# A fused attention and gate kernel: gate by exp and reciprocal in the last steps, a moved V group, an earlier K set, a split copy

## The chip, the cores and the metric

The kernel runs on one core of a Trainium2 chip. Its time is that of one execution in device microseconds, as the median of several runs. Every engine works through its own instructions in order: PE (TensorE, matrix products), ACT (ScalarE), DVE (VectorE), POOL (GpSimd) and SP (which only issues DMAs here).

## The reference

For one sequence of 2048 rows of width 512, with 32 heads of 16 and an inner width of 1376:

```python
xn = _layernorm(x, axis=-1)
s = _A_ref(xn, A_wqkv, A_wo)           # 32 heads: softmax(q k^T / 4) v, then @ wo
h = _gelu(jnp.einsum("bsd,df->bsf", xn, w1) + b1)
g = _silu(jnp.einsum("bsf,fd->bsd", h, w2) + b2)
return x + s * g
```

All is fp32. `silu(y)` is `y / (1 + exp(-y))`.

## The kernel before

**Precision.** Most products are made of three: each operand is split into a high part (rounded by an ACT copy) and a low part (the rest, by a subtraction on POOL or DVE), and high x high, high x low and low x high are added up in PSUM (`mm3`, L73 to 79, and `terms`).

**Work units.** The 2048 rows are 16 token tiles of 128 (`t`), or four chunks of 512 (`c`). Heads go in eight groups of four. A unit `u` is one head group and one chunk of queries, so there are 32 units of 16 key tiles each, that is 512 attention steps (`n`).

**First part (to about 57 us).** Layer norm, transposes, the first Q and K rows, and one V tile per chunk.

**Stage one (about 57 to 490 us).** A list (`plan`, L238 to 257) is built by a small planner and then carried out. Its entries are: three groups of four V tiles (`quad`), then up pairs and Q/K pairs, each in two halves (`half`), with the down products of finished up tiles between them (`down`). `half` accumulates a pair in the banks `ps_x` and `ps_m` and hands it to `evac` (gelu or copy on ACT, the split on ACT and POOL). `BANKS` says which PSUM pools a V group takes. When a chunk's down products are complete, its four gate tiles are copied to `gt` (L571) and put in `chores` and `silu`. `chore` adds `b2` on POOL. `gate` (L584 to 593), called behind the next Q/K pair, applies Silu to the four tiles on ACT and stores them to `g_d` in DRAM from POOL's queue; a gelu on a dummy element follows. Gelu, Silu, Exp and Sqrt each need a table in ACT, and the build puts a table load ahead of a function whose table is not there. The last chunk's four tiles are stored without Silu.

**Scores, for the softmax's maximum.** A score tile (S, `s_one`, L161 to 180) is one matmul of 48 rows into a bank of `s_tile` and a maximum over its 512 columns on DVE (L175). Each unit has 64 of them. In stage one `fill` (L466) puts S between the other matmuls, so that `4 * LEAD` of the 2048 S are done at its end. The rest are spread over the attention steps: `due(n)` (L791) says how many must be done by step `n`, in one straight line up to step `KBACK` and in a second one up to step `DONE`; 768 are due at `KBACK`. `KBACK` is thus the step from which the fourth K set (head group 3) is used, which is loaded into the place of the first in two halves, at steps 57 and 64, from POOL's queue.

**Attention steps (about 490 to 1619 us).** Each step makes four score products again (T, `t_one`, L691), now with the maximum subtracted inside the product, takes exp of each on ACT (L700), and multiplies the previous step's four results with V (V, `pv_step`, L702 to 716, eight matmuls). The order of T, S and V in a step is written out by hand for each number of S (`ORDER`, L39):

```python
ORDER = {0: "TTTTV", 1: "TTTTSV", 2: "TTTSTSV", 3: "STTTSTSV", 4: "STTSTSVTS"}
```

T uses four PSUM banks in turn, S three, V one. Behind the last V of a unit its result is copied out of that one bank to `os` (L712 to 716); the next unit's first V needs the bank. `o_move`, `o_den` and `o_div` then bring the sums to the denominators' place, take their reciprocals on DVE (L734), spread them through DRAM and divide (L744; on POOL, for the last unit on DVE).

`at(n, f, ...)` (L784) hangs further work on a step: loads of Q and K, `load_gx` (a token tile's `g` and `x`, from SP's queue, into four buffers `gx`), `w_token` (the split of a token tile's attention result), `w_mul` (its product with `wo`, four times 3 matmuls over two steps) and `w_out` (L776: times `g` on DVE, plus `x` on POOL, stored by SP). From step `DONE` on (490) there are no S any more, and the token tiles 0 to 10 are finished there, two steps each. Behind the loop come tile 11 (`spare`) and the last chunk's four, `T3` = 12 to 15. Two of those have their result split by chunk (`w_chunk`) in steps 509 and 511. In the tail the last unit is divided, and Silu is applied to the `g` of tiles 12 to 15 on ACT (L860 to 868).

Of the kernel before, what the change touches and what calls it, by code (L numbers as in the profile page):

```python
# [8 lines left out]
F32 = mybir.dt.float32  # L9
# [7 lines left out]
P = 128  # L17
# [14 lines left out]
VW = DH + 1  # L32
LEAD = 140
DONE = 490
KBACK = 70
FILL0 = 84
# [4 lines left out]
XB = 6  # L41
BANKS = ("ttvt", "xmtt", "ttvt")


@with_exitstack
def fused(ctx: ExitStack, tc: tile.TileContext, x, wqk, wv, wo, w1, b1, w2, b2, out):
# [101 lines left out]

    halves = [[(u, st, p) for u in range(NU) for st in range(NCH * NCH) for p in range(2)] for _ in range(2)]
    made = [0, 0]  # L150
# [86 lines left out]
    is_m = [pair[0][0] == "m" for pair in pairs]  # L237
    plan, nd = [("first", g) for g in range(VQ)], 0  # L238
    for j in range(len(pairs)):
        for h in range(2):  # L240
            plan.append(("half", j, h))
            ready = 4 * sum(is_m[:j])
            due = next((i for i in range(j, len(pairs)) if is_m[i]), len(pairs))
            nxt = next((i for i in range(j + h, len(pairs)) if is_m[i]), len(pairs))
            left = 2 * (nxt - j) + 1 - h
            need = 4 * sum(is_m[:nxt]) - 4 - nd
            room = 2 * (due + 1 - j) - h
            n = 2 if nd < len(parts) and parts[nd][2] and ready - nd > room else 1
# [290 lines left out]

    PA, silu, chores = {}, [], []  # L540

    def down(c, f, part):
# [22 lines left out]
        if f == FT - 1:  # L565
            for t in range(NCH):
                gt = wk.tile([P, D], F32, name="gt", bufs=4)
                if c == NCH - 1:
                    nc.vector.tensor_add(gt, PA[c][t], b2_sb)
                else:  # L570
                    nc.scalar.activation(gt, PA[c][t], AF.Copy)  # L571
                    chores.append(gt)
                rs = slice(c * CH + t * P, c * CH + (t + 1) * P)
                if c < NCH - 1:
                    silu.append((gt, rs))
                else:
                    nc.gpsimd.dma_start(g_d[rs, :], gt)

    def chore():
        if chores:  # L580
            gt = chores.pop(0)
            nc.gpsimd.tensor_add(gt, gt, b2_sb)

    def gate():  # L584
        while chores:
            chore()
        if not silu:
            return
        while silu:
            gt, rs = silu.pop(0)  # L590
            nc.scalar.activation(gt, gt, AF.Silu)
            nc.gpsimd.dma_start(g_d[rs, :], gt)
        nc.scalar.activation(junk, ident_r[:1, :1].bitcast(F32), AF.Gelu_apprx_tanh)

# [5 lines left out]
    def half(j, h):  # L600
# [5 lines left out]
        else:  # L606
            run((terms(y, 0, False), terms(x, 1, False)), {2: [lambda: w1_load(j + 2), errand], 10: [chore]})
            evac((x, y), PH)
            if x[0] == "q":
                gate()  # L610

    def quad(n):
# [4 lines left out]
        for i in range(4):  # L617
            hooks = {6: [mark]} if i in (1, 2) else {}
            if n == VQ - 1 and i in (0, 2):
                hooks[3] = [lambda: w1_split(0) if i == 0 else w1_load(1)]  # L620
# [81 lines left out]
    def pv_step(u, k):  # L702
# [8 lines left out]
        if k == NT - 1:  # L711
            OS[u] = wb.tile([P, CH], F32, name="os", bufs=1)  # L712
            if u < NU - 1:
                nc.scalar.activation(OS[u], PV.pop(u), AF.Copy)  # L714
            else:
                nc.vector.tensor_copy(OS[u], PV.pop(u))

# [27 lines left out]

    GX, OTS, PW = {}, {}, {}

    def load_gx(t):
        GX[t] = wb.tile([P, 2, D], F32, name="gx", bufs=4)
        nc.sync.dma_start(GX[t][:, 0], g_d[t * P:(t + 1) * P, :])  # L750
        nc.sync.dma_start(GX[t][:, 1], x[t * P:(t + 1) * P, :])

    def w_round(blocks, src, lo):
# [60 lines left out]
    for t in range(spare):  # L814
        n = DONE + 2 * t
        at(n - 4, load_gx, t)
        at(n - 2, w_token, t)
        at(n, w_mul, t, KS[:2])
        at(n + 1, w_mul, t, KS[2:])
        at(n + 1, w_out, t, nc.gpsimd)  # L820
    at(L - 4, load_gx, spare)
    at(L - 2, w_token, spare)
    for i, t in enumerate(T3[:2]):
        at(L - 3 + 2 * i, load_gx, t)
        at(L - 3 + 2 * i, w_chunk, i, nc.vector if i else nc.gpsimd)
    for k in range(KT):
        at(104 + 16 * k, load_wo, k)
        at(112 + 16 * k, split_wo, k)
# [76 lines left out]
```

## Time and profile before

| | |
|---|---|
| time, median of 3 runs | 1650.65 us (1649.59 to 1656.22) |
| time of the profiled execution | 1649.32 us |
| its span, first to last instruction | 1647.2 us |
| granted TensorE clock, mean | 0.996 |
| PE busy | 1624.7 us (99%) |
| DVE busy | 1371.6 us (83%) |
| ACT busy | 1284.8 us (78%) |
| POOL busy | 366.6 us (22%) |

The profile records one execution. A row of it names a line of the kernel, an engine, an operation, the tile written and those read, and the durations. Times in rows are microseconds from the span's start. Where rows of the same kind follow each other they are merged, with their count behind an x; what stands in brackets is the idle time of the engine ahead of the row and the instruction that ended it. PE's rows overlap, as matmuls are pipelined, so the distance from start to start is the measure there.

### The profile page before, as it was taken

To read this page: it belongs to the slowest core of one execution; us is meant where nothing else is said; L and a number is where in the kernel's file an instruction comes from. 1 tells how busy PE (TensorE), PEld (TensorE's weight loads), DVE (VectorE), ACT (ScalarE), POOL (GpSimd) and SP (SyncE) were. 2 spreads that over 40 slices of the span, in tenths; PEclk is the share of its full clock that TensorE was granted. 3 is DMA by queue.
4 is the path that set the end of the run, shared out by engine and by line. 5 is a ranking of instruction groups with operands and counts; after the bars stand their busy time and mean duration, and the time that the engine had idled before them with its cause. 6 is when DMAs were issued, how large, how long until landed. Compare 5 with 4: busy or idle time off the path is not lost.

```text
span 1647.2 us, 30938 instructions
## 1 busy us (share of the span) xinstructions
PE 1624.7 (99%) x11624; PEld 891.4 (54%) x11624; DVE 1371.6 (83%) x2256; ACT 1284.8 (78%) x2564; POOL 366.6 (22%) x360
## 2 busy tenths in 40 slices
PE   8999999999999999999999999999999999999997
PEld 7889989989984333333333343433333333433444
DVE  7289989999988888888888888988888888888612
ACT  4333443543539999999999999999999999999874
POOL 4145565756640011001000100100100000000143
PEclk9999999999999999999999999999999999999999
DMA  5635333463431122111411411411141111110243
GB/s 199 130 89 149 107 120 104 131 165 93 133 116 35 28 48 50 28 43 38 70 31 27 70 38 28 63 34 29 38 62 28 28 28 40 29 29 21 75 131 133
DMA packets 76069, 116.82 MB, mean 71 GB/s; under 512 B 24948, under 2 KB 25972, under 8 KB 74552
## 3 DMA queue, kind: packets, MB, share of 16 engines
q1 hardware_dynamic: 72464, 102.30, 22.9%
q0 software_dynamic: 3264, 12.35, 4.3%
q8 instruction: 92, 1.51, 0.4%
q14 instruction: 57, 0.47, 0.1%
q10 hardware_dynamic: 192, 0.20, 0.0%
HBM read 84.35 MB, written 25.97 MB: 67 GB/s over the span
## 4 chain that ended last, share of the span: by engine, by line
PE 93%; ACT 2%; DVE 1%; DMA 1%; issue 1%; POOL 1%; SPq 0%; ACTq 0%; DVEq 0%; POOLq 0%
PE pv L708 30%; PE ps L173 25%; PE ps L491 11%; PE pst L698 11%; PE pst L491 7%; PE ps L698 3%; PE ps L76 3%; PE pv L491 2%; ACT slot L700 1%; PE pst L76 1%; DMA xt<-in_x 0%; DMA raw<-in_wqk 0%; DMA gx<-in_x 0%; DVE slot L71 0%; PE ps L366 0%
## 5 line engine op out<-in xcount | busy, mean ns | idle before, releaser
L175 DVE TENSOR_REDUCE mx<-ps 128x1 f32<-128x512 f32 x2048 | 1306.5, 684 | 178.9 <-PE ps L173 68.1
L700 ACT ACTIVATE slot<-pst 128x512 f32<-128x512 f32 x1536 | 840.4, 611 | 44.2 <-PE pst L698 22.2
L708 PE MATMUL pv<-slot,vsb 128*32 128x512 f32 x4096 | 545.2, 604 | 1.4 <-ACT os L714 1.3
L173 PE MATMUL ps<-kt,slot 48*128 48x512 f32 x1024 | 368.2, 441 | 0.0
L698 PE MATMUL pst<-qt,kt 50*128 50x512 f32 x1152 | 358.8, 434 | 0.7 <-ACT slot L700 0.2
L173 PEld LDWEIGHTS ps<-kt,slot 48*128 48x128 f32 x1024 | 185.6, 184 | 275.0 <-DVE mx L175 256.6
L700 ACT ACTIVATE slot<-ps 128x512 f32<-128x512 f32 x512 | 312.6, 611 | 10.0 <-PE ps L173 1.9
L491 PE MATMUL ps<-slot,w1h 64*128 64x512 f32 x1088 | 227.9, 397 | 3.6 <-ACT junk L501 2.7
L173 PE MATMUL ps<-kt,qz 48*128 48x512 f32 x512 | 210.4, 415 | 0.3
L698 PEld LDWEIGHTS pst<-qt,kt 50*128 50x128 f32 x1152 | 162.3, 185 | 44.2 <-ACT slot L700 16.9
L173 PE MATMUL ps<-slot,slot 48*128 48x512 f32 x512 | 185.7, 438 | 0.0
L708 PEld LDWEIGHTS pv<-slot,vsb 128*32 128x32 f32 x4096 | 80.6, 108 | 182.6 <-issue 169.9
L698 PE MATMUL ps<-qt,kt 50*128 50x512 f32 x384 | 165.4, 431 | 0.0
L491 PEld LDWEIGHTS ps<-slot,w1h 64*128 64x128 f32 x1088 | 153.6, 186 | 15.7 <-ACT junk L501 5.6
L173 PEld LDWEIGHTS ps<-slot,slot 48*128 48x128 f32 x512 | 93.2, 184 | 126.4 <-DVE mx L175 117.0
L491 PE MATMUL ps<-slot,w1l 64*128 64x512 f32 x544 | 151.2, 395 | 0.0
L301 POOL TENSOR_TENSOR hl<-hg,hh 128x512 fp32r<-128x512 f32 x76 | 96.9, 1297 | 134.0 <-ACT hh L300 89.6
L698 PE MATMUL pst<-qt,slot 50*128 50x512 f32 x384 | 118.7, 432 | 0.0
L188 POOL TENSOR_TENSOR nmh<-nm,nmh 128x16 fp32r<-128x16 f32 x32 | 7.1, 222 | 492.4 <-DVE nm L187 364.2
L501 ACT ACTIVATE junk<-ident_r 1x1 f32<-1x1 f32 x95 | 18.6, 196 | 118.1 <-PE pv L491 74.9
L173 PEld LDWEIGHTS ps<-kt,qz 48*128 48x128 f32 x512 | 94.1, 184 | 11.8 <-DVE mx L175 3.4
L491 PEld LDWEIGHTS ps<-slot,w1l 64*128 64x128 f32 x544 | 85.1, 187 | 4.1
(143 smaller groups left out, 1648.9 us busy)
## 6 DMA issues: line engine op xcount, KB each, us to landing
raw<-in_w SPq DMA_DIRECT2D x88, 256.0 KB
qk_h<-hh SPq DMA_DIRECT2D x32, 256.0 KB
qk_l<-hl SPq DMA_DIRECT2D x32, 256.0 KB
qt<-qk_h SPq DMA_DIRECT2D x128, 64.0 KB
slot<-qk_h SPq DMA_DIRECT2D x96, 64.0 KB
xt<-in_x SPq DMA_DIRECT2D x16, 256.0 KB
g_d<-gt POOLq DMA_DIRECT2D x16, 256.0 KB, 4.2
qt<-qk_l SPq DMA_DIRECT2D x64, 64.0 KB
```

Of the source, the lines that this page charges most:

```text
L76: nc.tensor.matmul(ps, lhs[a], rhs[b], start=first and n == 0, stop=last and n == 2)
L173: nc.tensor.matmul(ps, q[r, p, qi * P:(qi + 1) * P], kts[g % KB][p][r, ki * CH:(ki + 1) * CH], start=True, stop=True)
L175: nc.vector.tensor_reduce(MX[u][:, 2 * p + a, qi, ki:ki + 1], ps, axis=AX.X, op=OP.max)
L188: nc.gpsimd.tensor_sub(NM[u][:, 1], nm, NM[u][:, 0].bitcast(F32))
L301: nc.gpsimd.tensor_sub(hl, raw, hh.bitcast(F32))
L491: i = nc.tensor.matmul(ps, lhs[r], rhs[r], start=first, stop=last).ins
L501: i = nc.scalar.activation(junk, ident_r[:1, :1].bitcast(F32), AF.Copy).ins
L698: nc.tensor.matmul(ps, kts[g % KB][p][r, k * P:(k + 1) * P], QT[u][r, p, :], start=True, stop=True)
L700: nc.scalar.activation(PT[u, k][:, 2 * p + a, :], ps, AF.Exp, scale=SCALE)
L708: nc.tensor.matmul(PV[u][32 * j:32 * j + 32, :], vsb[:, k, h:h + 32], PT[u, k][:, j, :], start=(k == 0), stop=(k == NT - 1))
```

## The change

1. `LEAD` 140 to 145 (580 S instead of 560 in stage one) and `KBACK` 70 to 64. The unit that first uses the fourth K set does its S in another order: first all that need the first half of the key columns.
2. Two of the three V groups come ahead of the first up pair, the third behind it. The second group takes its banks in another order.
3. The gates are no longer finished in stage one: `chore` adds `b2` and stores at once, and Silu is gone. Instead, `gate(t)` in the last steps computes `g / (1 + exp(-g))` per token tile: exp on ACT into one of four buffers (by `t % 4`), then plus one, reciprocal and product on DVE. It is hung on the step of `w_token` for tiles 0 to 11, on steps 505 and 507 for tiles 12 and 13, and on the tail for 14 and 15, between `o_den` and `w_out(spare)`. The `gx` of tiles 12 and 13 gets places of its own (in slots that held a K set) and is loaded in steps 501 and 503, that of tile 14 in step 511, that of tile 15 in the tail.
4. The copy at the end of a unit is half on ACT, half on DVE, for all units.

```diff
-LEAD = 140
+LEAD = 145
 DONE = 490
-KBACK = 70
+KBACK = 64
...
-BANKS = ("ttvt", "xmtt", "ttvt")
+BANKS = ("ttvt", "xtmt", "ttvt")
...
-    halves = [[(u, st, p) for u in range(NU) for st in range(NCH * NCH) for p in range(2)] for _ in range(2)]
+    def score_order(u):
+        tiles = list(range(NCH * NCH))
+        return sorted(tiles, key=lambda st: st % NCH // 2) if u == NCH * KB else tiles
+
+    halves = [[(u, st, p) for u in range(NU) for st in score_order(u) for p in range(2)] for _ in range(2)]
...
-    plan, nd = [("first", g) for g in range(VQ)], 0
+    plan, nd = [("first", g) for g in range(VQ - 1)], 0
     for j in range(len(pairs)):
         for h in range(2):
             plan.append(("half", j, h))
+            if j == 0 and h == 1:
+                plan.append(("first", VQ - 1))
...
                 else:
                     nc.scalar.activation(gt, PA[c][t], AF.Copy)
-                    chores.append(gt)
                 rs = slice(c * CH + t * P, c * CH + (t + 1) * P)
                 if c < NCH - 1:
-                    silu.append((gt, rs))
+                    chores.append((gt, rs))
...
     def chore():
         if chores:
-            gt = chores.pop(0)
+            gt, rs = chores.pop(0)
             nc.gpsimd.tensor_add(gt, gt, b2_sb)
-
-    def gate():
-        while chores:
-            chore()
-        if not silu:
-            return
-        while silu:
-            gt, rs = silu.pop(0)
-            nc.scalar.activation(gt, gt, AF.Silu)
             nc.gpsimd.dma_start(g_d[rs, :], gt)
-        nc.scalar.activation(junk, ident_r[:1, :1].bitcast(F32), AF.Gelu_apprx_tanh)
...
             evac((x, y), PH)
-            if x[0] == "q":
-                gate()
...
-            if n == VQ - 1 and i in (0, 2):
+            if n == VQ - 2 and i in (0, 2):
                 hooks[3] = [lambda: w1_split(0) if i == 0 else w1_load(1)]
...
-            if u < NU - 1:
-                nc.scalar.activation(OS[u], PV.pop(u), AF.Copy)
-            else:
-                nc.vector.tensor_copy(OS[u], PV.pop(u))
+            pv = PV.pop(u)
+            nc.scalar.activation(OS[u][:, :CH // 2], pv[:, :CH // 2], AF.Copy)
+            nc.vector.tensor_copy(OS[u][:, CH // 2:], pv[:, CH // 2:])
...
+    def spare_slot(i):
+        while len(spares) <= i:
+            spares.append(slot(len(spares), (P, KT, D)))
+        return spares[i]
+
     def load_gx(t):
-        GX[t] = wb.tile([P, 2, D], F32, name="gx", bufs=4)
+        if t in T3[:2]:
+            i = 2 * T3.index(t)
+            GX[t] = spare_slot(1)[:, i:i + 2]
+        else:
+            GX[t] = wb.tile([P, 2, D], F32, name="gx", bufs=4)
         nc.sync.dma_start(GX[t][:, 0], g_d[t * P:(t + 1) * P, :])
         nc.sync.dma_start(GX[t][:, 1], x[t * P:(t + 1) * P, :])
+
+    def gate(t):
+        e, g = spare_slot(0)[:, t % NCH], GX[t][:, 0]
+        nc.scalar.activation(e, g, AF.Exp, scale=-1.0)
+        nc.vector.tensor_scalar_add(e, e, 1.0)
+        nc.vector.reciprocal(e, e)
+        nc.vector.tensor_mul(g, g, e)
...
         at(n - 2, w_token, t)
+        at(n - 2, gate, t)
...
     at(L - 2, w_token, spare)
+    at(L - 2, gate, spare)
     for i, t in enumerate(T3[:2]):
-        at(L - 3 + 2 * i, load_gx, t)
+        at(L - 11 + 2 * i, load_gx, t)
+        at(L - 7 + 2 * i, gate, t)
         at(L - 3 + 2 * i, w_chunk, i, nc.vector if i else nc.gpsimd)
+    at(L - 1, load_gx, T3[2])
...
     w_chunk(2, nc.vector)
-    load_gx(T3[2])
+    load_gx(T3[3])
     for k in KS[1:-1]:
         for t in T3:
             w_mul(t, (k,))
-    for t in T3[:2]:
-        nc.scalar.activation(GX[t][:, 0], GX[t][:, 0], AF.Silu)
     o_den(NU - 1)
+    for t in T3[2:]:
+        gate(t)
     w_out(spare, nc.gpsimd)
-    load_gx(T3[3])
-    nc.scalar.activation(GX[T3[2]][:, 0], GX[T3[2]][:, 0], AF.Silu)
     o_div(NU - 1, nc.vector)
     w_chunk(KT - 1, nc.vector)
-    nc.scalar.activation(GX[T3[3]][:, 0], GX[T3[3]][:, 0], AF.Silu)
```

More of the change, by code (lines that the diff above doesn't have):

```diff
@@ L538, in terms @@
         return out
-    PA, silu, chores = {}, [], []
+    PA, chores = {}, []
     def down(c, f, part):
@@ L744, in o_div @@
         eng.tensor_mul(ot[c][rs, g // 2], ot[c][rs, g // 2], DN.pop(u)[rs])
-    GX, OTS, PW = {}, {}, {}
-    def load_gx(t):
-        GX[t] = wb.tile([P, 2, D], F32, name="gx", bufs=4)
+    GX, OTS, PW, spares = {}, {}, {}, []
+    def spare_slot(i):
+        while len(spares) <= i:
+            spares.append(slot(len(spares), (P, KT, D)))
+        return spares[i]
+    def load_gx(t):
+        if t in T3[:2]:
[3 more added lines that the diff above has]
+            GX[t] = wb.tile([P, 2, D], F32, name="gx", bufs=4)
         nc.sync.dma_start(GX[t][:, 0], g_d[t * P:(t + 1) * P, :])
         nc.sync.dma_start(GX[t][:, 1], x[t * P:(t + 1) * P, :])
+    def gate(t):
[4 more added lines that the diff above has]
+        nc.vector.tensor_mul(g, g, e)
     def w_round(blocks, src, lo):
```

## The prediction

> **What bounds the kernel now.** I read the page first, then busy time by stage, then the instructions in order of time around each place that the change touches.
>
> ```profile
> PE 1624.7 (99%) x11624; PEld 891.4 (54%) x11624; DVE 1371.6 (83%) x2256; ACT 1284.8 (78%) x2564; POOL 366.6 (22%) x360
> ...
> L175 DVE TENSOR_REDUCE mx<-ps 128x1 f32<-128x512 f32 x2048 | 1306.5, 684 | 178.9 <-PE ps L173 68.1
> ```
> ```profile
> 57.00:489.60 432.60, 427.98 (x3529) 385.14 (x3525) 374.02 (x578) 175.34 (x386) 236.29 (x201) 1.00 0.42 118
> 489.60:1619.30 1129.70, 1127.73 (x7766) 452.14 (x7765) 952.99 (x1580) 1076.24 (x2116) 101.81 (x128) 1.00 0.20 45
> 1551.00:1619.30 68.30, 68.30 (x379) 31.68 (x378) 7.07 (x11) 49.49 (x97) 29.02 (x24) 1.00 0.36 116
> 1619.30:1647.20 27.90, 18.36 (x84) 12.53 (x82) 9.94 (x14) 7.54 (x12) 6.33 (x5) 0.89 0.41 135
> ```
> In the second fence the columns are the stretch, its length, then PE, weight loads, DVE, ACT and POOL, then the granted clock and the DMA share. PE is never out of work before 1619 us, so a gain must shorten PE's own sequence or remove one of its waits. In the attention steps (489.6 to 1619) ACT is also at 95% and DVE at 84%. In the part from 1551 on, where the scores are done, DVE is nearly idle: 7.07 of 68.30 us. That idle room is where the new gates go. In the last 28 us PE waits on others for a third of the time: there the chain counts, not the sum of work.
>
> The profiled execution took 1649.3 us for a span of 1647.2; the median of the runs is 1650.65. I sum against 1649.3. A measurement of this kernel can tell about 0.5% (8 us) from no change.
>
> **1. Fewer steps with four score tiles (LEAD, KBACK).** From the formula of the due scores: before, 20 of the steps hold four score tiles (S), 2 hold two; after, 2 hold four and 4 hold two. Twenty S move to stage one. One four-S step, with the start of its value matmuls (V) and the ones beside it:
> ```profile
> 1273.76 1.06 PE L708 MATMUL pv<-slot,vsb 128*32 128x512 f32 x8
> 1275.64 1.06 PE L708 MATMUL pv<-slot,vsb 128*32 128x512 f32 x8
> 1278.37 1.07 PE L708 MATMUL pv<-slot,vsb 128*32 128x512 f32 x8
> ```
> ```profile
> 1217.67 1.06 PE L708 MATMUL pv<-slot,vsb 128*32 128x512 f32 x8
> 1219.80 1.07 PE L708 MATMUL pv<-slot,vsb 128*32 128x512 f32 x8
> 1222.11 1.07 PE L708 MATMUL pv<-slot,vsb 128*32 128x512 f32 x8
> 1224.23 1.06 PE L708 MATMUL pv<-slot,vsb 128*32 128x512 f32 x8
> ```
> A plain step takes 2.12 us (1222.11 to 1224.23). Around the four-S step two periods take 4.61 instead of 4.25: 0.36 us more. Eighteen fewer: **-6.5 us**. The fourth K set is then wanted six steps earlier. Its first half is issued at step 57 and the second at 64, and the new order of score tiles uses the first half alone for 32 tiles, over ten steps:
> ```profile
> 608.84 1.08 POOL L105 DMA_DIRECT2D kt<-qk_h  x2 [11.66 <-PE pst L698]
> ...
> 625.88 0.55 POOL L105 DMA_DIRECT2D kt<-qk_h  x1 [3.66 <-PE pst L698]
> ```
> ```profile
> kt<-qk_h POOLq DMA_DIRECT2D x8, 128.0 KB, 4.3
> ```
> The first row is step 57, the second step 64. The six pieces of the first half issue within some 3 us and land 4.3 us later, by about 616 us, 10 us ahead of step 64. It hides.
>
> **2. The end-of-unit copy.** The middle pair of V starts above (1219.80 to 1222.11) stands behind this:
> ```profile
> 1219.05 0.63 ACT L714 ACTIVATE os<-pv 128x512 f32<-128x512 f32 x1
> 1219.52 1.62 ACT L700 ACTIVATE slot<-pst 128x512 f32<-128x512 f32 x3
> ```
> The copy takes an ACT place of 0.47 us that the exponentials miss, and PE pays 2.31 - 2.12 = 0.19 us per unit. A half copy must cost less on ACT; the other half comes behind three reductions, three times 0.684 of a step's 2.12 us, on DVE. At 30 units the bounds are -5.7 and, if that half (about 0.4) finds no room on DVE, +6. I take **-5.7**: the three score buffers let DVE run late by a step, and a shorter ACT place fits where 0.47 just failed to.
>
> **3. Stage one.**
> ```profile
> 90.00:100.00 10.00, 8.76 (x71) 6.95 (x70) 8.10 (x13) 4.40 (x9) 3.79 (x3) 1.00 0.33 95
> 230.00:240.00 10.00, 7.81 (x61) 6.79 (x59) 6.65 (x11) 6.80 (x12) 7.99 (x9) 0.90 0.63 213
> 240.00:250.00 10.00, 10.00 (x83) 9.41 (x81) 8.97 (x14) 3.63 (x8) 5.09 (x4) 0.93 0.17 53
> 290.00:300.00 10.00, 10.00 (x90) 9.59 (x87) 9.71 (x16) 4.28 (x10) 6.11 (x6) 1.00 0.49 159
> ```
> ```profile
> 229.98 1.28 ACT L591 ACT_TABLE_LOAD   x1
> 231.28 2.19 ACT L591 ACTIVATE gt<-gt 128x512 f32<-128x512 f32 x4
> 233.49 1.28 ACT L593 ACT_TABLE_LOAD   x1
> ```
> PE starts about 88 matmuls per 10 us where nothing is late (90 in the last row): 0.114 us each. At 90 to 100, where two up pairs follow each other, 17 are missing: 1.9 us, which the third V group now fills. At 230 to 250 some 32 are missing (3.6 us) behind two table loads and four Silu, ahead of the next weight split on ACT, and the granted clock falls to 0.90 and 0.93. Without Silu I take 3.0 of it; the two other gates of this stage cost PE nothing that shows. The twelve additions and stores on POOL stay as many; each store now comes directly behind its addition. With the V group the first w2 split, a w2 load and the requests for K and Q go behind the first up pair; the first down part still has an up pair ahead of it, so none of them is late. Twenty S more at 0.114: +2.3. Sum **-2.6 us**, between -5.5 (all holes closed) and +8 (S bound by DVE, twenty times 0.684, less the hole at 230).
>
> **4. The gates, in the last steps.** Each of the 16 tokens gets exp on ACT, then an addition, a reciprocal and a product on DVE. No 128x512 reciprocal stands in the trace. The nearest rows:
> ```profile
> L734 DVE RECIPROCAL dr<-dr 128x16 f32<-128x16 f32 x32 | 7.8, 243 | 0.0
> L350 DVE RECIPROCAL ve<-ve 128x4 f32<-128x4 f32 x4 | 0.7, 178 | 1.1 <-ACT ve L349 1.1
> L352 DVE TENSOR_TENSOR ve<-ve 128x4 f32<-128x4 f32 x4 | 0.7, 162 | 0.1
> L357 DVE TENSOR_SCALAR xn<-xt,mv,ve 128x512 f32<-128x512 f32 x16 | 7.8, 548 | 0.1
> L778 DVE TENSOR_TENSOR gx<-ps,gx 128x512 f32<-128x512 f32 x15 | 10.3, 689 | 63.8 <-PE ps L76 47.1 <-DMA qt<-mh_d 6.2 <-issue 5.7
> L779 DVE TENSOR_TENSOR gx<-gx 128x512 f32<-128x512 f32 x2 | 2.5, 1252 | 0.1
> ```
> Twelve more elements cost the reciprocal 65 ns, 5.4 ns each, where the plain operation pays (689 - 162)/508 = 1.04. So 512 elements take 178 + 508 x 5.4 = 2.9 us; the bounds are 0.7 (as the plain operation) and 4.3 (65 ns for each group of eight, 64 groups). I take 2.9, since both rows lie on one line with the fixed 158 ns (162 less four times 1.04). The addition is 0.55 (L357), the product between 0.69 and 1.25 (L778, L779, the latter beside POOL): 0.95. One gate holds DVE for **4.45 us**, hand-overs included.
>
> The Trainium skill, "VectorE: DVE Perf Modes", section "First, the fixed hardware budget", says that a reciprocal is an iterated divide with a repeat count of 8. At its 0.96 GHz that would be an estimated 4.3 us for 512 elements; the rows above rise by less, and the sum by it is the first rival's.
>
> The g and x loads of tokens 12 and 13 go from steps 509 and 511 to 501 and 503 on SP's queue, into slots that no other tile uses by then: they wait for no buffer, and I count nothing for them. DVE takes its instructions in order, and the built order shows what comes behind the gates.
> ```profile
> 1547.43 0.65 ACT L757 ACTIVATE oh<-slot 128x512 fp32r<-128x512 f32 x1
> ```
> ```profile
> 1547.85 0.40 PE L173 MATMUL ps<-kt,slot 48*128 48x512 f32 x1
> 1604.76 1.07 PE L708 MATMUL pv<-slot,vsb 128*32 128x512 f32 x8
> 1608.01 1.06 PE L708 MATMUL pv<-slot,vsb 128*32 128x512 f32 x8
> ```
> ```profile
> 1604.97 0.65 ACT L757 ACTIVATE oh<-ot 128x512 fp32r<-128x512 f32 x1
> ```
> (a) Gate 0 (step 488) stands ahead of the last five score reductions. Its exp ends about 1548.5 (behind the copy at 1547.43), the gate at 1552.95, the next reduction at 1553.65. With three score buffers PE's third S of step 489 (before: 1547.85) waits for it: **+5.8**.
> (b) Gate 4 (step 496) stands ahead of DVE's new half of the end-of-unit copy, which the next V needs. By step 506: copy 1604.97, exp ends 1606.05, gate 1610.5, half copy about 0.45: 1610.95 instead of 1608.01: **+2.95**.
> (c) exp writes one of four buffers, by token modulo four. Tokens 12 and 13 (steps 505, 507) follow tokens 8 and 9 by one step only, so ACT, with all exponentials behind it, waits for DVE's product. On the times of (b): gate 8 is done at 1610.5, and ACT is ready for token 12 at 1608.2 (there is no copy in odd steps): 2.3 us. Then DVE does gate 12, a product and gate 9, to 1620.7, and ACT is ready for token 13 at 1608.2 + 6.5 + 1.3 = 1616.0: 4.7 us. ACT has about 0.9 us free per step (18.8 us idle in the 21 steps from 1551 on), so PE sees 1.3 and 3.6: **+4.9**.
> (d) Between the V of step 504 (6.5 us ahead of 1604.76) and the last copy of the value sums lie 24.85 us:
> ```profile
> 1623.11 0.69 DVE L716 COPY os<-pv 128x512 f32<-128x512 f32 x1 [0.50 <-PE pv L708]
> ```
> With (c) it is 29.75. DVE gets six gates and five short operations there, 30.2 us, from 1.3 us behind that V on, with one gap of 0.65: 32.15. The copy is late by **+2.4**.
> (e) In the tail:
> ```profile
> 1629.33 0.25 DVE L734 RECIPROCAL dr<-dr 128x16 f32<-128x16 f32 x1
> 1633.84 0.69 DVE L744 TENSOR_TENSOR ot<-ot,dn 64x512 f32<-64x512 f32 x1 [3.72 <-DMA dn<-den_d]
> ```
> ```profile
> 1631.15 0.86 ACTq L739 DMA_DIRECT2D dn<-den_d  x2
> ```
> The division follows the reciprocal's end by 4.26 us. After: 1.5 until ACT may issue its two loads, 0.86 to issue them, 0.6 for exp, two gates (8.9), the spare's product (0.69), all ahead of the division: 12.55, **+8.3**.
> The tail's removed Silu and its table load ran in that same DMA wait: nothing.
> (f) Behind the wait at 233 us the granted clock cost 10 x 0.10 + 10 x 0.07 = 1.7 us; two such at (a) and (e): **+3**.
> Together +27.4, so 1649.3 - 6.5 - 5.7 - 2.6 + 27.4 = **1662 us**.
>
> **Rivals.**
> *Reciprocal in groups of eight* (4.3 us; the two rows allow it, their common line speaks against it): each gate 5.85. (a) and (b) +1.4 each, (c) and (d) about +4 each, as their gates stand in a row, (e) +2.8: 1676 us. Chance 0.15.
> *A reciprocal near one element per cycle* (the other side): a gate of 2.25 us. (a) 3.6, (b) 0.75, (c) and (d) nothing, (e) 3.9: 8.2, so 1643 us. It decides below about 1.5 us per reciprocal, where, between 8.2 and 27.4, the loss falls under the 14.8 gained. The step from 178 to 243 ns speaks against it. Chance 0.12.
> *The waits overlap*: while PE stands at (a) to (c), DVE catches up, and (d) and (f) vanish along with half of (c): a loss of 19.5, 1654 us. Chance 0.13.
> *The fourth K set is late* at step 64, or S bound by DVE in stage one: 1670 us. Its loads have 10 us to spare. Chance 0.05.
>
> **The numbers.** The forecast has 0.55 and spans 1653 to 1670 with items 2 and 3 at their other values. The range reaches to both reciprocal cases: 1643 to 1677. Slower by over 0.5% (above 1658.9): two thirds of 0.55, and 0.15 + 0.05: 0.57. Faster (below 1642.4): 0.10, nearly all from the second rival. Within: 0.33.
>
> **What would show it.** The mean of the 128x512 reciprocal: 2.9, 4.3 or 0.7 us. V to V of 2.12 us with no four-S bumps and no 2.31 at the ends of units. No hole in PE at 90 to 100 and 230 to 240. A PE hole of 5 to 6 us at step 489, one of 3 us behind step 496, waits of ACT for a DVE product at steps 505 and 507, and 12 us between the last small reciprocal and the division. I am wrong if the reciprocal is short, or if gates overlap PE's work more than DVE's order allows.

## The result, and the profile after

The changed kernel takes **1693.47 us** in the median of its runs (1692.70 to 1694.19), beside 1653.43 for the kernel before on the same chip: 1.0241 of it, with a 95% interval of 1.0208 to 1.0273. It is slower by 2.4%, 31 us above the forecast of 1662 us and 16 us above the end of its range. The direction was as forecast, the size was not: 12.7 us were forecast, and between the two profiled executions there are 44. The profiled execution took 1693.36 us for a span of 1691.6.

The page of the kernel after, first its engines, then two of its groups (columns: line, engine, operation, names and shapes, count | busy us, mean ns | idle time before, and what ended it):

```profile
PE 1646.8 (97%) x11624; PEld 911.2 (54%) x11624; DVE 1456.5 (86%) x2335; ACT 1271.0 (75%) x2554; POOL 367.5 (22%) x360
...
L179 DVE TENSOR_REDUCE mx<-ps 128x1 f32<-128x512 f32 x2048 | 1303.6, 685 | 163.2 <-PE ps L177 62.7
...
L177 PEld LDWEIGHTS ps<-kt,slot 48*128 48x128 f32 x1024 | 187.6, 185 | 301.9 <-DVE mx L179 280.3
```

DVE has 85 us more work than before (1456.5 against 1371.6); PE 22 more, for the same 11624 matmuls. The last row says that the weight loads of these score tiles stand still for 280 us in all, because a score buffer is not yet reduced by DVE. They belong to the attention steps. The score tiles of stage one read `qz`, and most of them are in a row of their own. On the page of the kernel before, the two rows are these:

```profile
L173 PEld LDWEIGHTS ps<-kt,slot 48*128 48x128 f32 x1024 | 185.6, 184 | 275.0 <-DVE mx L175 256.6
...
L173 PEld LDWEIGHTS ps<-kt,qz 48*128 48x128 f32 x512 | 94.1, 184 | 11.8 <-DVE mx L175 3.4
```

Such a wait of the weight loads is not yet a loss of PE: on that page the matmuls that belong to the first row (L173 on PE) have no idle time ahead of them, and in the steps from 64 to 448 ACT is busy 804 of 831.7 us as well (below). And for stage one, where the change lost 10 us, the second row has 3.4 us of waiting for DVE, which gives no hint. What paces that stage is left to the experiments.

Busy time by stage tells where the 44.4 us of span went. The stretches are: stage one, the first 64 attention steps, steps 64 to 448, steps 448 to 511, the tail. Columns as in the prediction. The kernel before:

```profile
57.00:489.70 432.70, 428.07 (x3529) 385.14 (x3525) 374.12 (x578) 175.34 (x386) 236.39 (x201) 1.00 0.42 118
489.70:627.50 137.80, 137.61 (x956) 55.40 (x957) 121.84 (x203) 133.44 (x262) 10.89 (x19) 1.00 0.18 43
627.50:1459.20 831.70, 830.14 (x5799) 328.61 (x5796) 742.19 (x1230) 804.27 (x1583) 56.24 (x80) 1.00 0.20 40
1459.20:1619.30 160.10, 159.88 (x1013) 68.13 (x1012) 88.86 (x149) 138.53 (x273) 34.58 (x30) 1.00 0.25 75
```

Its tail is the last row of the windows in the prediction. The kernel after:

```profile
57.00:499.50 442.50, 440.58 (x3559) 394.03 (x3555) 385.74 (x600) 160.26 (x364) 236.95 (x203) 1.00 0.41 116
499.50:637.60 138.10, 137.27 (x957) 55.66 (x957) 121.13 (x202) 133.27 (x263) 10.96 (x19) 1.00 0.19 42
637.60:1466.20 828.60, 824.38 (x5781) 332.35 (x5779) 738.62 (x1238) 801.33 (x1582) 56.02 (x79) 1.00 0.20 40
1466.20:1651.70 185.50, 172.58 (x1014) 73.23 (x1011) 153.79 (x190) 144.91 (x287) 31.77 (x27) 0.93 0.23 68
1651.70:1691.60 39.90, 20.61 (x84) 13.99 (x82) 22.50 (x24) 5.34 (x10) 9.87 (x7) 0.78 0.24 80
```

Up to step 0 it is 9.8 us later (forecast: 2.6 earlier). Steps 0 to 448 gain 2.8 (forecast: 12.2). The last steps lose 25.4 and the tail 12.0, 37.4 together (forecast: 27.4). The three misses, 12.4 + 9.4 + 10.0, make up the 31 us.

The new gates, by the groups of the stretch from 1540 us on:

```profile
L758 DVE RECIPROCAL slot<-slot 128x512 f32<-128x512 f32 x16 | 53.6, 3353 | 0.5
...
L757 DVE TENSOR_SCALAR slot<-slot 128x512 f32<-128x512 f32 x16 | 14.7, 918 | 22.9 <-ACT slot L756 22.7
L759 DVE TENSOR_TENSOR gx<-gx,slot 128x512 f32<-128x512 f32 x14 | 9.7, 693 | 0.9
```

A reciprocal takes 3.35 us (2.9 was taken), the addition 0.92 (0.55), the product 0.69 (0.95): 4.97 in place of 4.45. The last number of the second row matters as much: DVE stood at the head of its queue for 22.7 us waiting for exp, with other work queued behind. DVE's order of time around step 488 shows both (start, duration, instruction, and in brackets its wait):

```profile
1552.32 1.29 DVE L179 TENSOR_REDUCE mx<-ps 128x1 f32<-128x512 f32 x2 [0.24 <-PE ps L691]
1555.48 1.14 DVE L757 TENSOR_SCALAR slot<-slot 128x512 f32<-128x512 f32 x1 [1.87 <-ACT slot L756]
1556.65 3.35 DVE L758 RECIPROCAL slot<-slot 128x512 f32<-128x512 f32 x1
1560.04 0.69 DVE L759 TENSOR_TENSOR gx<-gx,slot 128x512 f32<-128x512 f32 x1
1560.65 2.48 DVE L179 TENSOR_REDUCE mx<-ps 128x1 f32<-128x512 f32 x4
```

And PE in the same kernel, at the places (a), (b), (c) and (e) of the prediction:

```profile
1561.39 0.79 PE L177 MATMUL ps<-kt,slot 48*128 48x512 f32 x1 [6.53 <-DVE mx L179]
...
1596.75 1.93 PE L701 MATMUL pv<-slot,vsb 128*32 128x512 f32 x8 [3.27 <-DVE os L708]
...
1631.03 0.98 PE L691 MATMUL pst<-qt,kt 50*128 50x512 f32 x2 [1.42 <-ACT slot L693]
...
1641.88 1.47 PE L691 MATMUL pst<-qt,kt 50*128 50x512 f32 x3 [1.53 <-ACT slot L693]
...
1679.30 0.79 PE L76 MATMUL ps<-wo_h,oh 128*128 128x512 f32 x1 [11.96 <-ACT oh L765]
```

Each wait stands where it was forecast: 6.5 us (5.8 forecast), 3.3 (2.95), 1.4 and 1.5 (1.3 and 3.6). What was priced too low is what follows them. The same matmuls take 0.79 us, or eight V take 1.93, where they took 0.4 and 1.06. The windows behind the waits, with the granted clock as the third number from the end:

```profile
1558.00:1571.80 13.80, 10.41 (x33) 4.12 (x33) 9.48 (x11) 3.65 (x8) 1.50 (x2) 0.51 0.00 0
1571.80:1595.60 23.80, 21.69 (x117) 10.36 (x115) 17.63 (x13) 17.92 (x36) 8.01 (x6) 1.00 0.30 101
1595.60:1602.40 6.80, 5.65 (x18) 2.52 (x18) 1.62 (x3) 2.95 (x6) 1.57 (x2) 0.50 0.29 80
1633.20:1636.60 3.40, 3.40 (x14) 1.53 (x13) 3.33 (x4) 2.22 (x5) 1.12 (x1) 0.50 0.69 174
1643.40:1646.80 3.40, 3.40 (x7) 2.00 (x7) 3.37 (x2) 3.40 (x7) 1.28 (x1) 0.50 0.67 231
1670.70:1684.40 13.70, 5.10 (x12) 3.64 (x12) 11.16 (x12) 0.63 (x1) 3.05 (x2) 0.50 0.08 31
```

Each wait is followed by 3.4 to 13.7 us at half clock. Half of the time in which PE worked there is lost: (10.4 + 5.7 + 3.4 + 3.4 + 5.1) / 2 = 14 us, by the busy column, where 3 were forecast. (This is an estimate; no run takes the clock away and leaves the waits.) The Trainium skill, "TensorE: Matmul & The Clock Gate", "Part 1: The HAM clock gate", says that the clock falls to half after an idle window of about 3.4 us and comes back after a busy one. The steps of 3.4 us agree. The threshold does not: here waits of 1.42 and 1.53 us were enough, and the measurement decides. Nor is a wait of that length always followed by half clock: in the kernel with added DVE copies (below) waits of PE of 1.41 and 1.58 us, at 218 and 333 us, were not. The length varies too. The same wait of 6.5 us is followed by 13.7 us at half clock in two of these kernels and by 10.2 in five.

### The profile page after: what moved, and what is told of

The parts are those of the page before. It is cut to its first block, busy times and chain, and to the rows that moved or that the text cites. A ratio compares the mean times of both kernels' runs of the same rounds, so it can differ in the third digit from the quotient of the medians.

```text
span 1691.6 us, 31026 instructions
## 1 busy us (share of the span) xinstructions
PE 1646.8 (97%) x11624; PEld 911.2 (54%) x11624; DVE 1456.5 (86%) x2335; ACT 1271.0 (75%) x2554; POOL 367.5 (22%) x360
## 4 chain that ended last, share of the span: by engine, by line
PE 86%; issue 4%; ACT 4%; DVE 3%; POOL 1%; DMA 1%; SPq 0%; ACTq 0%; POOLq 0%; DVEq 0%
PE pv L701 27%; PE ps L177 24%; PE ps L497 12%; PE pst L691 8%; PE pst L497 7%; ACT slot L693 3%; PE ps L691 3%; PE pv L497 2%; PE ps L76 2%; PE pst L76 1%; DVE os L708 1%; DVE mx L179 1%; POOL ol L766 1%; POOL gx L787 1%; ACT os L707 1%
## 5 line engine op out<-in xcount | busy, mean ns | idle before, releaser
L497 PE MATMUL ps<-slot,w1h 64*128 64x512 f32 x1088 | 236.4, 396 | 0.3 <-ACT junk L507 0.3
L177 PE MATMUL ps<-kt,qz 48*128 48x512 f32 x512 | 217.9, 428 | 1.0 <-ACT mh L208 0.9
L691 PEld LDWEIGHTS pst<-qt,kt 50*128 50x128 f32 x1152 | 160.5, 186 | 35.4 <-ACT slot L693 14.4
L177 PE MATMUL ps<-slot,slot 48*128 48x512 f32 x448 | 159.9, 441 | 0.1
L177 PEld LDWEIGHTS ps<-slot,slot 48*128 48x128 f32 x448 | 81.8, 185 | 122.7 <-DVE mx L179 113.7
L736 POOL TENSOR_TENSOR ot<-ot,dn 64x512 f32<-64x512 f32 x15 | 19.3, 1286 | 351.1 <-DMA dn<-den_d 307.9
```

The lines of the kernel that those rows point to most:

```text
L177: nc.tensor.matmul(ps, q[r, p, qi * P:(qi + 1) * P], kts[g % KB][p][r, ki * CH:(ki + 1) * CH], start=True, stop=True)
L497: i = nc.tensor.matmul(ps, lhs[r], rhs[r], start=first, stop=last).ins
L691: nc.tensor.matmul(ps, kts[g % KB][p][r, k * P:(k + 1) * P], QT[u][r, p, :], start=True, stop=True)
L736: eng.tensor_mul(ot[c][rs, g // 2], ot[c][rs, g // 2], DN.pop(u)[rs])
```

## The experiments

Two theories stood against each other for each part. For the gates: DVE's hold (and the clock behind it) against ACT's exp and its buffers. For stage one: DVE paces it, against a cost of the moved V group. The time up to the first exponential of step 0 is read from each trace; eight kernels with the same stage one at LEAD 145 have it between 499.3 and 503.2 us, so a difference of up to 4 us there means nothing. Steps 448 to 511 take 182.6 to 185.5 us in the five kernels that have the same instructions there, as the spells at half clock differ in length; so a difference of 3 us there means nothing either. The times of whole kernels are medians. The changed kernel was not timed again beside the experiments; the kernel before took 1649.8 to 1651.6 beside these, and 1653.43 beside the changed kernel. Where the expectations name PE holes of 6.9, 2.0, 2.1 and 12.4 us, the wait in the rows above is 6.53, 1.42, 1.53 and 11.96.

### The gate left out, and the reciprocal left out

```diff
 def gate(t):
-    e, g = spare_slot(0)[:, t % NCH], GX[t][:, 0]
-    nc.scalar.activation(e, g, AF.Exp, scale=-1.0)
-    nc.vector.tensor_scalar_add(e, e, 1.0)
-    nc.vector.reciprocal(e, e)
-    nc.vector.tensor_mul(g, g, e)
+    pass
```

> The changed kernel with the body of the gate left out (the branch enters the product as stored, without x/(1+exp(-x))); loads, products and stores stay. Theory: the 37.3 us that the steps from 448 on and the tail lost come from the gates' instructions. Then these parts go back to about 160 and 27 us, and the whole takes 1656 us. Rival: half of it comes from what else moved there (loads of tokens 12 and 13 at other steps, the split copy): 1670 us or more.

Measured: 1656.83 us, 1.0035 of before (1.0023 to 1.0048). Steps 448 to 511 take 160.0 and the tail 28.8. So the gates cost 36.6 us, nearly all of the 37.4 that the end of the kernel lost; the loads and the split copy by themselves cost a microsecond there at most.

Only the line of the reciprocal taken out:

```diff
-    nc.vector.reciprocal(e, e)
```

> The changed kernel with the reciprocal left out of the gate (exp on ACT, addition and product on DVE stay, so the gate's value is another one). Theory: DVE's hold of 3.35 us by the reciprocal is what PE waits for. With about 1.6 us of DVE left per gate, less than the room that three score buffers give, the holes at steps 489 and 497 and those behind tokens 12 and 13 shrink to below 1 us each, and the whole is 1658 to 1662 us. Rival: it is the exp on ACT and the reuse of its four buffers that counts: 1680 us or more.

Measured: 1666.36 us, 1.0092 (1.0068 to 1.0116). The reciprocal is worth 27.1 of the 36.6 us. But 9.5 stay, more than the theory allowed. PE at step 489 in this kernel, and DVE ahead of it:

```profile
1561.52 0.50 PE L177 MATMUL ps<-kt,slot 48*128 48x512 f32 x1 [3.14 <-DVE mx L179]
```
```profile
1559.00 1.14 DVE L757 TENSOR_SCALAR slot<-slot 128x512 f32<-128x512 f32 x1 [1.87 <-ACT slot L756]
1560.17 0.69 DVE L758 TENSOR_TENSOR gx<-gx,slot 128x512 f32<-128x512 f32 x1
```

DVE's hold is 1.8 us here; as long again it waits for exp, which stands behind the exponentials on ACT. The cost of the gate is the wait of the first DVE operation and the work behind it, not the work alone.

### The gate of token 0 behind the last reductions: (a)

```diff
-        at(n - 2, gate, t)
+        at(n if t == 0 else n - 2, gate, t)
```

> The changed kernel with the gate of token 0 alone issued at step 490 instead of 488, behind the last score reductions. By the prediction's (a) this takes away a PE hole of 5.8 us; the trace shows one of 6.9 us, with the granted clock at half for 13.7 us from there. Theory that the clock loss belongs to the hole: both go, and the steps from 448 to 511 fall from 185.5 to about 173 us: 1681 us. Rival: DVE, with 4.97 us of gate for each 4.3 us of two steps, only hands the wait to the next gate; the hole turns up again behind token 1 or 2, and the whole stays above 1688.

Measured: 1683.30 us, 10.2 less than the changed kernel; steps 448 to 511 take 175.1, against 182.6 to 185.5 with the hole. So 7.5 to 10.4 us go with a hole of 6.5, and 1 to 4 of them belong to the clock behind it. The rival falls: the next hole is the one that was there already, only 0.6 us longer.

```profile
1551.00:1571.80 20.80, 20.58 (x119) 9.03 (x118) 17.86 (x21) 17.86 (x36) 5.57 (x6) 1.00 0.17 60
1586.30:1593.10 6.80, 6.06 (x22) 2.71 (x26) 1.52 (x4) 3.10 (x6) 1.99 (x2) 0.50 0.32 97
```

PE is busy and at full clock where the hole was; behind the V that waits for DVE's half copy the clock is still at half.

### The end-of-unit copy on ACT alone: the second part, and (b)

```diff
-            nc.scalar.activation(OS[u][:, :CH // 2], pv[:, :CH // 2], AF.Copy)
-            nc.vector.tensor_copy(OS[u][:, CH // 2:], pv[:, CH // 2:])
+            nc.scalar.activation(OS[u], pv, AF.Copy)
```

> The changed kernel with the end-of-unit copy of the first 31 units and the last on ACT alone. By the prediction's second part the split gained 0.19 us in each of 30 units, so this is 5.7 us slower: 1699 us. Rival: the half on DVE stands behind the score reductions and makes the next value matmul wait as long as the whole copy on ACT did: steps 0 to 448 stay within 2 us. In the last steps the copy no longer stands behind a gate on DVE, which gives back some 3 us at step 497 and 2 us at the last one: 1688 us.

Measured: 1685.57 us, 7.9 less than the changed kernel. Steps 64 to 448 and the last steps of this kernel:

```profile
638.90:1466.90 828.00, 826.46 (x5781) 329.45 (x5779) 733.07 (x1213) 803.87 (x1582) 55.96 (x79) 1.00 0.19 40
1466.90:1644.90 178.00, 168.39 (x1014) 71.65 (x1011) 150.54 (x187) 145.44 (x287) 33.08 (x28) 0.95 0.22 71
```

In steps 64 to 448 the split gained nothing: 828.0 without it, 828.6 with it. The trace of the changed kernel has the weight loads of V waiting 21.1 us for DVE's half; in this kernel they wait 12.2 for the whole copy on ACT, in the kernel before 12.0: one wait took the place of another. In the last steps the removal of the half copy brings 4.6 to 7.5 us (178.0 against 182.6 to 185.5): the hole of 3.3 at 1596.75 and the half clock behind it.

### A place of their own for tokens 12 and 13: (c)

```diff
-        e, g = spare_slot(0)[:, t % NCH], GX[t][:, 0]
+        e, g = spare_slot(2 if t in T3[:2] else 0)[:, t % NCH], GX[t][:, 0]
```

> The changed kernel with the exp of tokens 12 and 13 written into a slot of their own instead of the buffers of tokens 8 and 9. By the prediction's (c) ACT waits there for DVE's products and PE loses 4.9 us; the trace shows PE holes of 2.0 and 2.1 us behind ACT at 1631 and 1642, each with 3.4 us at half clock. Theory: both holes and the half clock go, about 6 us: 1687 us. Rival: DVE is behind by then whatever the buffers; the last half copy and the tail come as late as before, and the whole stays within 2 us of the changed kernel.

Measured: 1689.56 us, 3.9 less, which is within the scatter named above. Steps 448 to 511 fall from 185.5 to 178.1, but the tail grows from 39.9 to 43.1: neither theory alone. The two ACT holes are gone, and part is handed on: PE now waits 2.56 us at 1652.32 for a subtraction on POOL, which stands there behind an addition that waited 6.9 us for a product of DVE. The changed kernel's DVE has six gates and five short operations in a row up to the last half copy, which comes 2.3 us after ACT's half (1657.77 against 1655.45), as (d) of the prediction worked out.

### The last two gates left out: (e)

```diff
-    for t in T3[2:]:
-        gate(t)
```

> The changed kernel with the gates of tokens 14 and 15 left out (their branch enters the product as stored). By the prediction's (e) the two gates hold up the division by 8.3 us; with 4.97 us per gate it would be 9.3. Theory: PE's hole of 12.4 us in the tail falls to about 3, the clock at the end is higher, and the tail after step 511 falls from 39.9 to about 29 us: 1682 us. Rival: the tail is late because the gates of tokens 11 to 13 still stand ahead on DVE; it falls by less than 5 us.

Measured: 1683.31 us, 10.2 less; the tail is 29.9. In the changed kernel the division follows the end of the small reciprocal by 12.9 us (DVE, in order of time):

```profile
1664.61 0.25 DVE L726 RECIPROCAL dr<-dr 128x16 f32<-128x16 f32 x1 [1.32 <-DMA dr<-os]
1668.15 0.43 DVE L757 TENSOR_SCALAR slot<-slot 128x512 f32<-128x512 f32 x1 [3.29 <-ACT slot L756]
1668.61 3.35 DVE L758 RECIPROCAL slot<-slot 128x512 f32<-128x512 f32 x1
...
1677.77 0.69 DVE L736 TENSOR_TENSOR ot<-ot,dn 64x512 f32<-64x512 f32 x1
```

Without the two gates the division waits for its DMA alone:

```profile
1668.67 0.69 DVE L736 TENSOR_TENSOR ot<-ot,dn 64x512 f32<-64x512 f32 x1 [4.36 <-DMA dn<-den_d]
```

The four places together (10.2 + 7.9 + 3.9 + 10.2) give 32.2 of the gates' 36.6 us, each with some 3 us of scatter. The rest, (d) among it, was not tried by itself.

### LEAD at 140 and 130: the pace of stage one

```diff
-LEAD = 145
+LEAD = 140
...
+    last = 0
     for n in range(L + 1):
```

(`last` needs a value ahead of the loop because step 0 now begins with a score tile.)

> The changed kernel with LEAD back at 140, all else kept. Theory: stage one is paced by DVE, and each of the 20 further score reductions costs about 0.57 us there (11.5 us in all, read from the progress of the matmuls). Then the time from the start to the first exponential of step 0 falls from about 500 to 488 us; some 16 steps get a fourth score tile back (+0.36 us each, about +6): 1688 us. Rival: the moved V group, or the stores that follow it, make stage one slow, and a score tile costs only its 0.114 us on PE: stage one falls by 2.3 us alone, and the whole is 1697.

Measured: 1688.85 us. The first exponential of step 0 comes at 487.5 us, 12.1 earlier; the first 64 steps take 147.4, 9.4 longer (an estimated 3 of them by 6.8 us at half clock behind step 0, which the changed kernel does not have there). Twenty score tiles cost 0.6 us each in stage one, five times the 0.114 of the prediction, and the moved V group costs nothing that shows.

The same with 130:

```diff
-LEAD = 145
+LEAD = 130
```

> The changed kernel with LEAD at 130: 60 score tiles fewer in stage one, 56 of the first 64 steps with four. Theory that DVE's reductions are the bound on both sides: stage one falls by 60 x 0.57 = 34 us to about 466 us, unless PE's own work (some 3490 matmuls at 0.114 us from 57 us on) stops it at about 470; the first 64 steps take 64 x 3.875 x 0.684 = 170 us instead of about 137: the two cancel, and the whole stays within 5 us of the changed kernel. Rival, score tiles nearly free in stage one: it falls by 7 us there, pays 30 in the steps, and the whole is 1715 us or more.

Measured: 1702.31 us, 8.8 above the changed kernel where at most 5 were expected (the profiled execution, the fastest of the four, is 4.4 above). The first 64 steps take 171.1 (forecast 170), but stage one ends at 474.4, only 25 us earlier. That fits PE's own work as the limit there (the expectation put it at about 470), and the reductions no longer follow each other as closely (0.76 us apart); no run shows that limit by itself. Its stage one, its first 64 steps:

```profile
57.00:474.40 417.40, 415.89 (x3491) 372.29 (x3487) 352.16 (x538) 160.47 (x364) 236.65 (x201) 1.00 0.43 122
474.40:645.50 171.10, 165.48 (x1015) 65.98 (x1015) 157.06 (x263) 133.72 (x264) 11.27 (x20) 1.00 0.14 36
```

### One DVE operation more behind every fourth reduction of stage one

```diff
+        if "seen" in prog and sum(made) % 4 == 0:
+            nc.vector.tensor_copy(dj[:, 8:], dj[:, :8])
...
+    dj = keep_r.tile([P, 16], F32, name="dj")
+    nc.vector.memset(dj, 0.0)
```

> The changed kernel with one more DVE operation behind every fourth score reduction of stage one: a copy of 128x8 elements inside SBUF that nothing reads, 145 in all. The trace shows the smallest DVE operations of this stage at 160 to 220 ns, so this is 23 to 32 us more of DVE time, while DVE is idle for some 54 us of the stage (378.9 busy of 433). Theory that DVE's turn from one reduction to the next paces the stage: nearly all of it comes through, and the first exponential of step 0 comes 18 to 30 us later, at 518 to 530 us. Rival, PE paces the stage and a score tile costs its time there: the copies find room in DVE's idle time, and the stage is under 6 us longer.

Measured: 1730.36 us; the first exponential comes at 534.9, 35.4 us later. That is more than was expected, because the copies were dearer (groups of DVE in stage one, the kernel with the copies):

```profile
L179 DVE TENSOR_REDUCE mx<-ps 128x1 f32<-128x512 f32 x580 | 385.7, 687 | 55.5 <-PE ps L177 35.5 <-PE ps L499 10.0 <-PE pst L499 3.8
L181 DVE COPY dj<-dj 128x8 f32<-128x8 f32 x145 | 62.1, 428 | 0.0
```

DVE's busy time in the stage rises by 43.1 us (428.9 against 385.7; copies overlap their neighbours), and 35.4 of it come through, although DVE was idle for 57 us (442.5 less 385.7). PE, idle for 2 us of the stage in the changed kernel, is now idle for 21. The page's row for the weight loads of these score tiles says the same, 41.9 us of waiting for DVE where the changed kernel has 4.5:

```profile
L177 PEld LDWEIGHTS ps<-kt,qz 48*128 48x128 f32 x512 | 93.7, 183 | 53.6 <-DVE mx L179 41.9
```

The reductions of the changed kernel itself, in the same stage:

```profile
L179 DVE TENSOR_REDUCE mx<-ps 128x1 f32<-128x512 f32 x580 | 382.1, 689 | 63.1 <-PE ps L177 37.0 <-PE ps L497 11.1 <-PE pst L497 3.9
```

They start from 76.2 to 495.4 us, so one every 0.72 us, and one takes 0.69. With LEAD at 140 it is again one every 0.72 us (560 from 78.0 to 483.0). So DVE paces stage one from the first reduction on: 19 of its 57 idle us lie ahead of that reduction, most of the rest are short gaps between a reduction and the next score tile, and most of what is added to DVE there is paid.

### The gate by tanh

```diff
 def gate(t):
     e, g = spare_slot(0)[:, t % NCH], GX[t][:, 0]
-    nc.scalar.activation(e, g, AF.Exp, scale=-1.0)
-    nc.vector.tensor_scalar_add(e, e, 1.0)
-    nc.vector.reciprocal(e, e)
-    nc.vector.tensor_mul(g, g, e)
+    nc.scalar.activation(e, g, AF.Tanh, scale=0.5)
+    nc.vector.scalar_tensor_tensor(g, e, 1.0, g, op0=OP.add, op1=OP.mult)
...
-        nc.vector.tensor_mul(gx[:, 0], PW.pop(t), gx[:, 0])
+        nc.vector.scalar_tensor_tensor(gx[:, 0], PW.pop(t), 0.5, gx[:, 0], op0=OP.mult, op1=OP.mult)
```

> The changed kernel with the gate as x(1+tanh(x/2))/2: tanh on ACT in place of exp, one DVE operation (t+1) times x in place of three, and the factor of one half put into the product with the value that DVE does anyway. DVE's hold per gate is then about 0.7 us instead of 4.97. If tanh stands in the table that the exponentials use, no table load appears: the steps from 448 on take about 161 us, the tail some 29, and the whole 1658 us, near the kernel without gates (1656.8). Rival: each tanh brings two table loads of 1.28 us on ACT, 32 in all; ACT has 18.8 us idle in the last steps, so some 25 us stay: 1680 us.

Measured: 1665.12 us, 1.0091 (1.0076 to 1.0106), 28 us less than the changed kernel. No table load stands behind the one at 498.94 us, ahead of step 0. The Trainium skill, "ScalarE: Activation LUTs", section "Table sets: the hidden batching unit", lists tanh in the set of exp, and the trace agrees. The kernel is 7 us above the forecast: 3.4 of them in stage one, within the scatter, and some 4 at step 489, where S again waits, 2.7 us, for a reduction behind the gate:

```profile
1560.75 0.50 PE L177 MATMUL ps<-kt,slot 48*128 48x512 f32 x1 [2.68 <-DVE mx L179]
```

### What was left of the change, and the opposite direction

The tanh gate, token 0's at step 490, the copy as before (ACT, the last one on DVE), LEAD 140 and KBACK 70; the V group and stage one without Silu as in the changed kernel (beside the tanh edits above):

```diff
-LEAD = 145
-KBACK = 64
+LEAD = 140
+KBACK = 70
...
-            nc.scalar.activation(OS[u][:, :CH // 2], pv[:, :CH // 2], AF.Copy)
-            nc.vector.tensor_copy(OS[u][:, CH // 2:], pv[:, CH // 2:])
+            if u < NU - 1:
+                nc.scalar.activation(OS[u], pv, AF.Copy)
+            else:
+                nc.vector.tensor_copy(OS[u], pv)
...
-        at(n - 2, gate, t)
+        at(n if t == 0 else n - 2, gate, t)
```

> What the runs so far leave of the change: the moved V group and stage one without Silu stay; LEAD 140 and KBACK 70 and the copy on ACT as before; the gates as tanh in the last steps, that of token 0 at step 490. Theory: stage one is 1.7 and 3.3 us shorter than before (the two closed holes), 485 us; steps 0 to 448 as before, 969.5; then 160.5 and a tail of 29: 1644 to 1646 us, 5 us faster than the kernel before. Rival: the closed holes are handed on to the next wait in a stage that DVE paces: stage one stays at 489 to 490 and the whole at 1650.

Measured: 1648.27 us, 0.9981 of before (0.9967 to 0.9994). Its last steps and tail show gates at no cost to PE in the steps:

```profile
1458.50:1618.60 160.10, 159.88 (x1013) 68.12 (x1012) 105.39 (x163) 145.65 (x287) 35.20 (x30) 1.00 0.25 81
1618.60:1647.80 29.20, 19.68 (x84) 13.31 (x82) 12.30 (x17) 4.99 (x9) 6.84 (x5) 0.89 0.31 100
```

DVE has 16.5 us more work in the first row than the kernel before, for the same 160.1 us. But stage one ends at 489.2, within a microsecond of before: the rival holds. The two holes are closed, and DVE, which sets the pace there, has as many reductions as ever. The kernel is faster than before by 0.2%, less than the 0.5% that the prediction set as a bound: no more than level with the kernel before.

The same with the tiles moved the other way than the change did:

```diff
-LEAD = 140
-KBACK = 70
+LEAD = 135
+KBACK = 77
```

> The same with LEAD 135 and KBACK 77: 20 score tiles leave stage one, the fourth K set is used 7 steps later instead of 6 earlier, and 41 instead of 20 of the later steps have four score tiles. Theory: a score tile costs about 0.6 us in stage one (12.1 for 20 of them, by LEAD 145 against 140), and a lone fourth one in a later step 0.18 to 0.36: -12 + 4 to 8, so 1637 to 1641 us. Rival: at 135 PE is already the bound of stage one and the tiles bring half of that there: 1645 or more.

Measured: 1652.45 us, 1.0003 (0.9991 to 1.0015). Stage one is 10.2 us shorter (forecast 12), but the first 64 steps lose 2.9 and steps 64 to 448 take 840.2 in place of 831.7: the 18 more steps with four score tiles there cost 8.5 us, 0.5 each, not 0.18 to 0.36. The 2.9 go with a spell of 6.8 us at half clock at 481.3, of which half would be 3.4. The kernel without gates has one like it at 502.7 and also takes 3 us longer there, while the changed kernel has none; so the 2.9 say nothing about score tiles. Score tiles cost about the same wherever they are put before step 490.

## Why the prediction was wrong

**1. Four-S steps, -6.5.** Half right. With the copy on ACT in both, steps 64 to 448 take 831.7 before and 828.0 with the earlier K set: -3.7, or 0.2 us for each of the 17 four-S steps that go from there, instead of 0.36. The 0.36 came from one place of the trace; in the other direction (LEAD 135) such a step costs 0.5, so there is no one price. The fourth K set was in time, as forecast.

**2. End-of-unit copy, -5.7.** Wrong: +0.6 in steps 64 to 448, which is nothing. The prediction named the other end (+6, if the half finds no room on DVE) and chose against it. The step that failed was "the three score buffers let DVE run late by a step": DVE's half stands behind reductions, and the weight loads of the next V wait 21.1 us for it, more than the 12.0 for the whole copy on ACT before.

**3. Stage one, -2.6.** Wrong by 12.4 us, the largest miss. Twenty tiles at 0.114 us was PE's price; DVE's was the one to take. LEAD alone shows 0.6 us per tile, and the added DVE operations show why. The bound "S bound by DVE, twenty times 0.684" stood in the text (+8, and 9.8 came), and as a rival with a chance of 0.05. The step that failed was taking "PE is never out of work" for "PE is the bound". The prediction's own window from 290 to 300 us shows PE busy for 10.00 us and DVE for 9.71: two full engines, and the work was added to both. The wait rows would not have told, as the weight loads of stage one wait 3.4 us for DVE in the kernel before. The holes at 90 and 230 us did close; by the two kernels with LEAD 140 (487.5 and 489.2 against 489.7), that bought 2.2 us at most, of the 4.9 forecast, and 2.2 is within the scatter of that stage.

**4. The gates, +27.4.** The places and the waits were right, and the sizes of (a), (b), (d) and (e) within a microsecond: 6.5 for 5.8, 3.3 for 2.95, 2.3 for 2.4; the division follows the reciprocal's end by 12.9 for 12.55. (c) was smaller in PE's waits (1.4 + 1.5 for 4.9). These waits make up 23.6 us, where (a) to (e) had 24.4. The reciprocal was 0.45 us longer than worked out from the two short rows, the addition longer beside POOL. What failed was (f): 3 us for the granted clock, priced at two holes from one place at 233 us, against some 14. Each of the five waits of the changed kernel had its tail at half clock, the small ones too, and 23.6 + 14 = 37.6 is within 0.2 us of what the end of the kernel lost. The removals carry the tail with them: 7.5 to 10.4 us for a hole of 6.5, 4.6 to 7.5 for one of 3.3.

**The rivals.** Neither short nor long reciprocal (3.35 us lies between 2.9 and 4.3). "The waits overlap" fell: taken away one by one they add up to 32.2 of 36.6, and the sum of the waits came out as forecast. "S bound by DVE in stage one" came in, on top of the forecast and not in place of it.

## What to carry to other kernels

Before a part is priced on the engine that looks full, see which other engine is nearly as full in that stage, and how closely its instructions follow one another. Here PE was busy for 10.00 and DVE for 9.71 of 10 us. The waits between the two came to a few microseconds, and still most of the work added to DVE was paid (35.4 of 43.1 us), while the holes closed on PE brought 2.2 us at most. An operation put on an engine that works in order costs its wait for its own input plus its length for all that is queued behind it. A stop of PE can cost more than itself: here stops of 1.4 to 6.5 us were followed by 3.4 to 13.7 us at half clock. A function that stands in the table already loaded (tanh beside exp here) can turn three operations of the pacing engine into one.

## What had not been expected of the hardware

- The fp32 reciprocal of 128x512 takes 3353 ns, 6.5 ns an element, in each of its 16 uses; the 128x16 one takes some 250 ns in the same kernel.
- Small DVE operations between SBUF tiles vary with POOL. The gate's addition takes 0.42 to 0.43 us in the four uses with no POOL tensor operation beside it (at 1668.15 for one) and up to 1.55 in the other twelve (1.14 at 1555.48, while a POOL subtraction of 1.27 us from 1555.07 runs). The 128x8 copies of the DVE experiment take 0.16 us in the 77 uses without one and up to 2.13 in the other 68, 428 ns in the mean of all. The reductions from PSUM keep to 685 ns.
- Waits of PE of 1.42 and 1.53 us were each followed by 3.4 us at half clock, and waits of 1.41 and 1.58 us in another kernel by none. Four kernels show a spell of 6.8 to 10.2 us at half clock just behind step 0, with no wait of PE above 0.8 us within 4 us ahead of it.
